# Identity products, idle rings and a lead for attention ahead of the first FFN tiles

## The chip, the cores and the metric

One NeuronCore of a Trainium2 chip runs the whole program. The metric is the device time of one execution in microseconds. TensorE is called PE in the profile (PEld for its weight loads), VectorE DVE, ScalarE ACT, GpSimd POOL and SyncE SP; SP here only issues DMAs.

## What is computed

Windowed attention with a few sink keys, then a mixing over the sequence and a two-layer FFN, for 4 batches of 768 positions with 8 heads of 64.

```python
scores = q @ k.T / 8                  # kept: the first 4 keys, and the last 128 up to the query
a = softmax(scores)                   # with 1e-9 added to the denominator
x = (a @ v) as [4, 768, 512]
h = x^T @ U @ V                       # U [768, 32], V [32, 768]
u = x + h^T
out = u + relu(u @ w_ch1) @ w_ch2     # w_ch1 [512, 2048], w_ch2 [2048, 512]
```

All arrays are fp32. Most products run in a faster fp32 format ("fp32r") on an operand split in two, a high part and the remainder, so that one fp32 product becomes three: weights as `w` (high and low), activations as `uh` and `ul`, hidden values as `hh` and `hl`. Some products of batch 0 and 1 run in plain fp32 on unsplit operands; the code calls those "whole" or "native".

## The kernel before

Rows are taken in blocks of 128 and in two chunks (halves) of 384 positions. The work of a batch:

- *Attention*, per head and half: scores (`scores`, L637 to L641) into a PSUM bank, mask and row minimum on DVE (L643), exponential with the row sum on ACT (L648), the division (`normalise`: `r` by L667 and L669, then the scaling L679 to L682), transposes of the probabilities (`transposes`, L701), and the values (`values`, L751), which end in `xT`, x with channels on the partitions.
- *Loads of v* (`prep_v`): for "whole" heads (all 16 of batch 0, all 8 of batch 1) v goes straight from memory into a buffer of the ring `vhl`, which has two.
- *Mixing*: when a half's heads are done, `mix_half` transposes each block of x (L865), copies it to `xf` (a helper's line, L462), multiplies it by U into the bank `tp` (L871) and stores it in `xd`, from where the FFN's last step fetches it. The ring `xf` has two buffers, shared with the first loads (hence the names first1q and first1k). `mix_end` then copies `tp` to `t` (L462, L912). For each chunk c and each of four channel groups d it forms the mixing in a bank, adds it to x and splits the sum into `uh` and `ul`. In batch 0 the contribution of the sink keys is a separate product (L922) into the same bank, ahead of the product with `t` (L925).
- *FFN* (`ffn`): per tile f of 128 hidden units, 12 products of `uh`, `ul` with `w` (L952 to L954), the ReLU split in `hh` and `hl` (L960, L963), and 9 products into three accumulating banks (L973). The accumulators start with the mixing itself (L990, in batch 0 with L987 ahead of it), so x alone is left to be added at the end (L999).
- *Weights*: each of the 16 tiles is split once, in batch 0. `narrow` takes a raw piece through a row of DVE and ACT steps (L94 to L102) and `weights` writes high and low part (L462, L469). Two tiles stay resident, the other 14 share four buffers and are written to memory and fetched back. In batch 0 the FFN goes through the tiles in groups of four, chunk 1 first (`FLIP = 1`), then chunk 0 with the same four backwards and the next four, and so on.

The order of the instructions on every engine is not written out. `Plan` schedules all steps on a model before anything is emitted: each step has a duration for each engine that may run it, a priority `prio`, and the tiles it reads and writes; of the ready steps the one with the lowest priority number goes first on a free engine. Where a step may run on several engines, `any` lets the plan choose, with the durations weighted by `PRICE`. The order is refined in up to ten rounds of a backward and a forward pass:

```python
for s in self.steps:
    s.prio = -s.back - s.lead
```

`lead` is what stands in `plan.lead` when a step is made: `LEAD0` for the attention and mixing of batch 0, 0 for the splitting of weights and the FFN, `LEAD` = 30 for the attention of later batches. Tile buffers come from rings: box i of a ring may be used once box i - n has been read for the last time, and its first step stands behind the first step of box i - 1. PSUM banks are a free pool of eight. All loads and stores go through SP's one queue in the plan's order.

Of the kernel before, what the change touches and what calls it, by code (L numbers as in the profile page):

```python
# [10 lines left out]
F32R = mybir.dt.float32r  # L11
# [10 lines left out]
P = 128  # L22
# [36 lines left out]
PERIOD = 4.32  # L59
ACC = (0xFFFF, 0xFFFF, 0xFFFF, 0xFFFF)  # L60
WHOLE = {0: (0xFFFF, 0xFFFF), 1: (0xFF, 0xFF)}
LEAD0 = 0.0
LEAD = 30.0
BESIDE = ((6, 2.5), (0, 2.5), (0, 2.5))
ORDER = (0, 1, 2, 3, 4, 5, 6, 7, 8, 9, 10, 11, 12, 13, 14, 15)
# [369 lines left out]
class Fast:  # L435
# [135 lines left out]
    def prep_v(self, b, h, blocks, t0, whole=False):  # L571

        nc, add = self.nc, self.plan.add
        k0, k1 = blocks
        n = k1 - k0
        src = lambda: self.v[b, h][:, k0:k1, :]
        if whole:
            t = self.vhl()
            flat = lambda: f32(t().rearrange("p n s d -> p (n s d)")[:, :(n + 1) * D])
            self.put(t, lambda: (flat().rearrange("p (n d) -> p n d", n=n + 1), self.v[b, h][:, k0:k1 + 1, :]), (n + 1) * 32768, t0 - 8)  # L580
            return t, flat, k0
        r, t = self.v_raw(), self.vhl()
        self.put(r, lambda: (r()[:, :n], src()), n * 32768, t0 - 8)
        self.copy(n * D, lambda: t()[:, :n, 0, :], lambda: r()[:, :n], r=(r,), w=(t,), prio=t0 + 3)
        self.tt(n * D, lambda: t()[:, :n, 1, :], lambda: r()[:, :n], lambda: f32(t()[:, :n, 0, :]), ALU.subtract,
                r=(r,), w=(t,), prio=t0 + 3)
        return t, None, k0
# [75 lines left out]
    def normalise(self, b, h, half, t0, acc, p, sm, psink):  # L663
        nc, add = self.nc, self.plan.add
        r = self.rr()
        if acc:
            add("DVE", 0.08, lambda: nc.vector.scalar_tensor_tensor(  # L667
                r(), sm(), 1e-9, sm(), ALU.add, ALU.max), r=(sm,), w=(r,), prio=t0)
        add("DVE", 0.09, lambda: nc.vector.reciprocal(r(), r() if acc else sm()), r=(sm,), w=(r,), prio=t0)  # L669
        kept = lambda: p()[:, :, SW:]  # L670
        by = lambda: r().unsqueeze(2).broadcast_to([P, NBLK, SW])
# [149 lines left out]
    def mix_half(self, b, half, t0):  # L821
# [38 lines left out]
        for blk in range(half * NBLK, (half + 1) * NBLK):  # L860
            xp = self.bank()

            def mms(xp=xp, blk=blk):
                for pr in range(NPAIR):
                    nc.tensor.transpose(  # L865
                        xp()[:, pr * P:(pr + 1) * P], xT[pr]()[:, blk * P:(blk + 1) * P], self.ident)
            add("PE", mm(P, NPAIR), mms, r=[(x, (half, i)) for x in xT for i in range(2)], w=(xp,), prio=t0)
            xf = self.xf()
            self.copy(DM, xf, xp, psum=True, r=(xp,), w=(xf,), prio=t0)
            if native:  # L870
                add("PE", mm(DM, 4), lambda blk=blk, xf=xf: nc.tensor.matmul(  # L871
                    tp(), self.usf()[:, blk, :], xf(),
                    start=blk == 0, stop=blk == NB - 1), r=(xf, self.T[b], self.usf), w=(tp,), prio=t0)
                xd = self.xd[b][blk]
                self.put(xd, lambda xd=xd, xf=xf: (xd(), xf()), 262144, t0, r=(xf,))
                continue
            xh, xl = self.xh(), self.xl()
            self.copy(DM, xh, xf, r=(xf,), w=(xh,), prio=t0)
            self.tt(DM, xl, xf, lambda xh=xh: f32(xh()), ALU.subtract, r=(xf, xh), w=(xl,), prio=t0)
            xd = self.xd[b][blk]  # L880
            self.put(xd, lambda xd=xd, xf=xf: (xd(), xf()), 262144, t0, r=(xf,))

            def st1(blk=blk, xh=xh, xl=xl):
                nc.tensor.matmul(tp(), self.ust()[:, blk, :], xh(), start=blk == 0, stop=False)
                nc.tensor.matmul(tp(), self.ust()[:, blk, :], xl(), start=False, stop=blk == NB - 1)
            add("PE", mm(DM, 2), st1, r=(xh, xl, self.T[b], self.ust), w=(tp,), prio=t0)
# [21 lines left out]
    def mix_end(self, b, t0):  # L908
# [5 lines left out]
        for c in range(NCHUNK):  # L914
            uh, ul = self.u[b, c] = self.uh(), self.ul()
            sl = slice(c * CH, (c + 1) * CH)
            for d in range(NC):
                pu, x = self.bank(), xT[d]
                parts = [(x, (c, j)) for j in range(2)]
                if b == 0:  # L920
                    pst, vs = self.late[3][c], self.late[4]
                    add("PE", mm(CH), lambda pu=pu, d=d, vs=vs, pst=pst: nc.tensor.matmul(  # L922
                        pu()[:, :CH], vs()[:, d, :], pst()[:, :CH], start=True, stop=False),
                        r=(vs, pst, x), w=(pu,), prio=t0)
                add("PE", mm(CH), lambda pu=pu, d=d, sl=sl: nc.tensor.matmul(  # L925
                    pu()[:, :CH], t()[:, d * P:(d + 1) * P], self.vst()[:, sl], start=b > 0, stop=True),
                    r=(t, self.vst), w=(pu,), prio=t0)
                add("DVE", dve(CH), lambda pu=pu, x=x, sl=sl: nc.vector.tensor_tensor(
                    x()[:, sl], x()[:, sl], pu()[:, :CH], ALU.add), r=(pu,), w=parts, prio=t0)
                top = lambda uh=uh, d=d: uh()[:, d, :]  # L930
# [5 lines left out]
    def ffn(self, b, c, fs, prio, first, begin=True, end=True):  # L936
# [40 lines left out]
        for i in range(n + 1):  # L977
            if i < n:
                l1(i)
            if i == 0:  # L980
                acc = [Box(lambda i: self.banks[i], self.accs[k:k + 1], ring=self.bank) for k in range(NBLK)]
                self.accs = acc
                for k in range(NBLK if begin else 0):
                    blk = c * NBLK + k
                    if b == 0:
                        pst, vs = self.late[3][c], self.late[4]
                        add("PE", mm(DM), lambda k=k, vs=vs, pst=pst: nc.tensor.matmul(  # L987
                            acc[k](), pst()[:, k * P:(k + 1) * P], vs().rearrange("p n d -> p (n d)"),
                            start=True, stop=False), r=(vs, pst), w=(acc[k],), prio=prio)
                    add("PE", mm(DM), lambda k=k, blk=blk: nc.tensor.matmul(  # L990
                        acc[k](), self.vst()[:, blk * P:(blk + 1) * P], self.T[b](), start=b > 0, stop=False),
                        r=(self.vst, self.T[b]), w=(acc[k],), prio=prio)
# [362 lines left out]
```

## Time and profile before

| | |
|---|---|
| time, median of 3 runs (lowest to highest) | 780.61 us (780.37 to 783.29) |
| the profiled execution | 780.66 us, span 778.9 us |
| busy share PE / DVE / ACT / POOL | 97% / 60% / 45% / 30% |
| granted TensorE clock, mean | 0.990 |
| DMA | 153.90 MB, mean 198 GB/s |

A busy PE is not PE at its peak, since matmuls are pipelined; rows of a timeline can overlap for that reason. The idle time before an instruction, in brackets, is put down to the semaphore event that came last; where the engine named had long been done, it was another, often a DMA. Helpers record many operations under one line (copies L462 and L463, elementwise L469 and L471), so such rows are told apart by their tiles.

### The profile page before, as it was taken

What the parts mean: (1) busy time and instruction counts of PE and PEld (TensorE: products, weight loads), DVE (VectorE), ACT (ScalarE), POOL (GpSimd) and SP (SyncE); (2) the same over time, 40 slices, a digit from 0 to 9 for tenths busy, and PEclk for the clock granted to TensorE, in tenths of its full rate; (3) what the DMA queues carried; (4) which work ended last, traced back from release to release, by engine and by line L of the source; (5) the groups of instructions that cost most, each with busy time, mean ns of one, the idle gap of its engine ahead of it and who ended that gap; (6) DMA issues with size and microseconds to landing.
All of it is one profiled execution on the core that took longest, in us unless ns stands there. A gap on an engine that the chain in (4) does not pass through costs nothing.

```text
span 778.9 us, 11763 instructions
## 1 busy us (share of the span) xinstructions
PE 754.1 (97%) x4004; PEld 668.9 (86%) x4004; DVE 468.8 (60%) x1205; ACT 352.7 (45%) x953; POOL 233.6 (30%) x332
## 2 busy tenths in 40 slices
PE   8897899999999999999999999999999999999996
PEld 6675788888888899999889998899999899898995
DVE  8999649889889767866864157676754131112111
ACT  6996327566567454645642144545642111111110
POOL 5662104222233444655811035356521000000000
PEclk9999799999999999999999999999999999999999
DMA  8797448785595729764477529853147536533652
GB/s 292 255 315 272 148 149 285 227 266 183 175 284 197 262 76 277 248 203 129 121 229 252 186 76 271 233 177 132 68 129 250 204 135 222 207 112 121 243 195 93
DMA packets 46981, 153.90 MB, mean 198 GB/s; under 512 B 5824, under 2 KB 13888, under 8 KB 37440
## 3 DMA queue, kind: packets, MB, share of 16 engines
q1 hardware_dynamic: 46752, 152.86, 59.8%
q8 instruction: 33, 0.54, 0.3%
q14 instruction: 36, 0.29, 0.1%
q10 hardware_dynamic: 160, 0.20, 0.1%
HBM read 123.42 MB, written 29.62 MB: 196 GB/s over the span
## 4 chain that ended last, share of the span: by engine, by line
PE 73%; DVE 15%; DMA 4%; ACT 4%; issue 2%; POOL 1%; SPq 0%; DVEq 0%; ACTq 0%; POOLq 0%
PE bank L973 29%; PE bank L952 10%; PE bank L954 10%; PE bank L953 10%; PE bank L751 4%; DMA qkraw<-in_q_dram 3%; DVE p L643 2%; PE bank L701 2%; DVE nr L99 2%; PE bank L637 1%; PE bank L640 1%; DVE bank L101 1%; DVE w L469 1%; PE bank L641 1%; DMA xd<-first1q 1%
## 5 line engine op out<-in xcount | busy, mean ns | idle before, releaser
L973 PE MATMUL bank<-w,hh 128*128 128x512 f32 x768 | 243.0, 398 | 0.0
L963 DVE SCALAR_TENSOR_TENSOR hl<-bank,hh 128x384 fp32r<-128x384 f32 x128 | 71.0, 554 | 197.9 <-ACT hh L960 197.3
L952 PE MATMUL bank<-ul,w 128*128 128x384 f32 x512 | 178.4, 348 | 0.3 <-DVE ul L469 0.2
L954 PE MATMUL bank<-uh,w 128*128 128x384 f32 x512 | 172.7, 337 | 0.0
L953 PE MATMUL bank<-uh,w 128*128 128x384 f32 x512 | 172.4, 337 | 0.0
L960 ACT ACTIVATE hh<-bank 128x384 fp32r<-128x384 f32 x114 | 55.9, 490 | 227.9 <-PE bank L954 227.0
L973 PEld LDWEIGHTS bank<-w,hh 128*128 128x128 f32 x768 | 139.9, 188 | 19.8
L973 PE MATMUL bank<-w,hl 128*128 128x512 f32 x384 | 152.0, 396 | 0.0
L648 ACT ACTIVATE p<-p,mn 128x260 f32<-128x260 f32 (+1 forms) x192 | 93.9, 491 | 48.8 <-DVE mn L643 48.0
L952 PEld LDWEIGHTS bank<-ul,w 128*128 128x128 f32 x512 | 96.4, 188 | 6.3 <-DVE ul L469 0.5
L953 PEld LDWEIGHTS bank<-uh,w 128*128 128x128 f32 x512 | 96.3, 188 | 5.6 <-DVE w L469 0.3
L471 POOL TENSOR_TENSOR p<-p 128x256 f32<-128x256 f32 (+1 forms) x48 | 42.4, 883 | 186.9 <-ACT p L648 186.3
L954 PEld LDWEIGHTS bank<-uh,w 128*128 128x128 f32 x512 | 96.1, 188 | 0.0
L973 PEld LDWEIGHTS bank<-w,hl 128*128 128x128 f32 x384 | 72.1, 188 | 17.0 <-DVE hl L963 0.3
L643 DVE CUSTOM_DVE_ANT_0 p<-bank,mask 128x260 f32<-128x260 f32 (+1 forms) x192 | 71.5, 400 | 24.2 <-PE bank L641 21.9
L751 PEld LDWEIGHTS bank<-oph,vhl 128*128 128x128 f32 x336 | 56.1, 193 | 16.0 <-POOL oph L726 3.8
L751 PE MATMUL bank<-oph,vhl 128*128 128x256 f32 (+1 forms) x336 | 62.8, 321 | 5.9 <-DVE nr L99 2.1
L726 POOL TENSOR_SCALAR_AFFINE_SELECT oph<-oph 128x384 f32<-128x384 f32 (+1 forms) x64 | 37.2, 582 | 22.9 <-ACT oph L462 19.7
L471 POOL TENSOR_TENSOR ul<-xT,uh 128x384 fp32r<-128x384 f32 x14 | 14.0, 1019 | 97.5 <-ACT uh L462 97.4
L701 PE MATMUL bank<-ident,p 128*128 128x128 f32 x192 | 34.3, 281 | 3.3 <-ACT p L679 2.5
L667 DVE SCALAR_TENSOR_TENSOR r<-sm 128x3 f32<-128x3 f32 x64 | 34.4, 538 | 4.8 <-ACT p L648 4.7
L701 PEld LDWEIGHTS bank<-ident,p 128*128 128x128 f32 x192 | 24.5, 142 | 13.9 <-ACT p L679 6.2
(171 smaller groups left out, 1077.8 us busy)
## 6 DMA issues: line engine op xcount, KB each, us to landing
w<-wd SPq DMA_DIRECT2D x60, 1024.0 KB, 4.9
big<-in_w_dram SPq DMA_DIRECT2D x32, 512.0 KB, 5.3
wd<-w SPq DMA_DIRECT2D x14, 1024.0 KB, 4.7
big<-xd SPq DMA_DIRECT2D x33, 256.0 KB, 3.7
qkraw<-in_q_dram SPq DMA_DIRECT2D x39, 192.0 KB, 5.0
qkraw<-in_k_dram SPq DMA_DIRECT2D x32, 198.0 KB, 4.9
out_dram<-big SPq DMA_DIRECT2D x24, 256.0 KB, 2.0
v_raw<-in_v_dram SPq DMA_DIRECT2D x16, 192.0 KB, 2.6
```

Of the source, the lines that this page charges most:

```text
L471: ways["POOL"] = (gps(n), lambda: nc.gpsimd.tensor_tensor(dst(), a(), b(), op), True)
L643: add("DVE", dve(wd), lambda st=st, u=u, lo=lo, wd=wd, qb=qb: nc.vector.tensor_tensor_reduce(p()[:, u, NS + lo:], st()[:, :wd], self.mask[ ...
L648: add("ACT", act(wd) + 0.22, lambda u=u, lo=lo: nc.scalar.activation(p()[:, u, NS + lo:], p()[:, u, NS + lo:], AF.Exp, bias=mn()[:, u:u + ...
L701: nc.tensor.transpose(tr()[:, u * P:(u + 1) * P], p()[:, u, SW + NS:], self.ident)
L726: add("POOL", 0.126 + CH * 0.914e-3, lambda t=t: nc.gpsimd.affine_select(as_(t()[:, :, 1, :]), f32(t()[:, :, 1, :]), [[0, NBLK], [1, P]], ...
L751: nc.tensor.matmul(out, st, f32(mv) if whole else mv, start=part == 0 and i == 0, stop=part == len(t) - 1 and i == len(mms) - 1, skip_grou ...
L952: nc.tensor.matmul(ph()[:, :CH], wh, ul()[:, d, :], start=d == 0, stop=False)
L953: nc.tensor.matmul(ph()[:, :CH], wl, uh()[:, d, :], start=False, stop=False)
L954: nc.tensor.matmul(ph()[:, :CH], wh, uh()[:, d, :], start=False, stop=d == NC - 1)
L960: self.plan.any({"ACT": (act(CH), lambda: nc.scalar.activation(hh(), ph()[:, :CH], AF.Relu)), "DVE": (dve(CH), lambda: nc.vector.tensor_sc ...
L963: add("DVE", dve(CH), lambda: nc.vector.scalar_tensor_tensor(hl(), ph()[:, :CH], 0.0, f32(hh()), ALU.max, ALU.subtract), r=(ph, hh), w=(hl ...
L973: nc.tensor.matmul(acc[k](), a()[:, sl], w()[:, m, :], start=not begin and i == 0 and j == 0, stop=i == n - 1 and j == 2)
```

## The change

There are seven edits, nearly all for batch 0.

1. `LEAD0` goes from 0 to 10.
2. The direct loads of v for odd heads go to the ring `opl` (two buffers), which holds the low part of transposed probabilities and stands idle while heads are "whole". This holds for batch 0 and for batch 1.
3. The step L667, `r` = row sum + 1e-9, may run on ACT, priced at 0.2 us, or on DVE, priced at 0.4 us instead of 0.08 and marked as one that shares a port with POOL.
4. In batch 0 the third block of each half (2 and 5) takes its `xf` from the ring `opl`.
5. In `mix_end` the sinks' product and the product with `t` become one step, so the first waits for `t` as well (batch 0, both chunks).
6. For batch 0's chunk 1 a product of x with the unit matrix (`ident`, plain fp32) opens the bank, with `tp` as an added dependency. `uh` is then copied from the bank and `ul` subtracted from it. x itself isn't updated.
7. In `ffn` the sinks' product into the accumulators (L987) waits for `T[b]`, the tile `t`.

```diff
-LEAD0 = 0.0
+LEAD0 = 10.0
@@ prep_v
-            t = self.vhl()
+            t = self.opl() if h % 2 else self.vhl()
@@ normalise
-            add("DVE", 0.08, lambda: nc.vector.scalar_tensor_tensor(
-                r(), sm(), 1e-9, sm(), ALU.add, ALU.max), r=(sm,), w=(r,), prio=t0)
+            self.plan.any({"ACT": (0.2, lambda: nc.scalar.activation(r(), sm(), AF.Copy, bias=1e-9)),
+                           "DVE": (0.4, lambda: nc.vector.scalar_tensor_tensor(
+                               r(), sm(), 1e-9, sm(), ALU.add, ALU.max), True)}, r=(sm,), w=(r,), prio=t0)
@@ mix_half
-            xf = self.xf()
+            if native and blk % NBLK == 2:
+                xf = self.opl(...)
+            else:
+                xf = self.xf()
@@ mix_end
-                if b == 0:
-                    pst, vs = self.late[3][c], self.late[4]
-                    add("PE", mm(CH), lambda pu=pu, d=d, vs=vs, pst=pst: nc.tensor.matmul(
-                        pu()[:, :CH], vs()[:, d, :], pst()[:, :CH], start=True, stop=False),
-                        r=(vs, pst, x), w=(pu,), prio=t0)
-                add("PE", mm(CH), lambda pu=pu, d=d, sl=sl: nc.tensor.matmul(
-                    pu()[:, :CH], t()[:, d * P:(d + 1) * P], self.vst()[:, sl], start=b > 0, stop=True),
-                    r=(t, self.vst), w=(pu,), prio=t0)
+                late = [self.late[4], self.late[3][c]] if b == 0 else []
+                early = b == 0 and c == FLIP
+                if early:
+                    add("PE", mm(CH, 4), lambda pu=pu, x=x, sl=sl: nc.tensor.matmul(
+                        pu()[:, :CH], self.ident, x()[:, sl], start=True, stop=False), r=parts + [tp], w=(pu,), prio=t0)
+
+                def run(pu=pu, d=d, sl=sl, late=late, early=early):
+                    if late:
+                        nc.tensor.matmul(pu()[:, :CH], late[0]()[:, d, :], late[1]()[:, :CH], start=not early, stop=False)
+                    nc.tensor.matmul(pu()[:, :CH], t()[:, d * P:(d + 1) * P], self.vst()[:, sl], start=not late, stop=True)
+                add("PE", mm(CH, 2 if late else 1), run, r=[t, self.vst] + late, w=(pu,), prio=t0)
+                if early:
+                    top, xs = lambda uh=uh, d=d: uh()[:, d, :], lambda pu=pu: pu()[:, :CH]
+                    self.copy(CH, top, xs, psum=True, r=(pu,), w=((uh, d),), prio=t0)
+                    self.tt(CH, lambda ul=ul, d=d: ul()[:, d, :], xs, lambda top=top: f32(top()), ALU.subtract,
+                            pool=False, r=(pu, (uh, d)), w=((ul, d),), prio=t0)
+                    continue
@@ ffn
-                            start=True, stop=False), r=(vs, pst), w=(acc[k],), prio=prio)
+                            start=True, stop=False), r=(vs, pst, self.T[b]), w=(acc[k],), prio=prio)
```

More of the change, by code (lines that the diff above doesn't have):

```diff
@@ L867, in mix_half @@
             add("PE", mm(P, NPAIR), mms, r=[(x, (half, i)) for x in xT for i in range(2)], w=(xp,), prio=t0)
-            xf = self.xf()
+            if native and blk % NBLK == 2:
+                xf = self.opl(lambda: f32(self.pool.tile([P, NBLK, 2, P], F32R, name="opl", bufs=NOP)).rearrange(
+                    "p n a b -> p (n a b)")[:, :DM])
+            else:
+                xf = self.xf()
             self.copy(DM, xf, xp, psum=True, r=(xp,), w=(xf,), prio=t0)
```

## The prediction

> **What bounds the kernel now.** I read the page's chain of waits first, then the engines' busy time by stage, and last the timeline of each engine around the start of the FFN. The chain that ended last looks settled: it is mostly TensorE's own.
>
> ```profile
> PE 73%; DVE 15%; DMA 4%; ACT 4%; issue 2%; POOL 1%; SPq 0%; DVEq 0%; ACTq 0%; POOLq 0%
> ```
>
> An average over stages hides the one that matters. The windows below cut the span at the points where the work changes: attention of batch 0 (10 to 71 us), its mixing (71 to 88), the first FFN tiles (88 to 110), FFN beside the rest of the weight splitting (110 to 262), and the rest. The columns are the length, then busy us and instructions for PE, PEld, DVE, ACT and POOL, the granted TensorE clock, and DMA.
>
> ```profile
> core 0 of [0], span 778.9 us
> core 0: us, PE busy (x) PEld busy (x) DVE busy (x) ACT busy (x) POOL busy (x), PEclk, DMA share, GB/s
> 10.00:71.00 61.00, 53.04 (x285) 43.53 (x285) 58.14 (x197) 53.81 (x170) 37.40 (x53) 0.97 0.86 295
> 71.00:88.00 17.00, 12.33 (x38) 8.16 (x37) 11.16 (x22) 7.37 (x15) 2.82 (x3) 0.70 0.74 268
> 88.00:110.00 22.00, 21.72 (x109) 19.39 (x109) 11.71 (x23) 5.39 (x11) 0.16 (x1) 1.00 0.12 43
> 110.00:262.00 152.00, 150.50 (x786) 131.62 (x785) 136.89 (x343) 99.02 (x252) 43.00 (x54) 1.00 0.73 235
> 262.00:779.00 517.00, 508.32 (x2764) 459.31 (x2762) 243.74 (x591) 182.45 (x495) 147.79 (x205) 1.00 0.55 179
> ```
>
> From 88 us on TensorE is the bound (508.3 of 517.0 us in the last window, the end of the span included). Work moved on other engines there is worth almost nothing. Before 88 us it is not: in 10 to 71 VectorE is 95% busy and ScalarE 88%, and in 71 to 88 nothing is full and the clock was only 0.70. So this change, nearly all of which lies in batch 0, is worth what it moves the first FFN product forward, less whatever TensorE work is only put off past that point.
>
> **The mixing, 71 to 88 us.** These are rows of TensorE's, ScalarE's, VectorE's and SyncE's timelines: start, us, engine, line, operation, and in brackets the idle time before.
>
> ```profile
> 73.88 0.60 PE L865 MATMUL bank<-ident,xT 128*128 128x128 f32 x4
> 79.00 0.69 PE L922 MATMUL bank<-xhl,vsh 128*128 128x384 f32 x1 [3.44 <-DVE w L469]
> 79.49 1.91 PE L871 MATMUL bank<-first1k,xT 128*128 128x512 f32 x2
> 88.22 0.44 PE L952 MATMUL bank<-ul,w 128*128 128x384 f32 x1
> ```
>
> ```profile
> 77.64 0.59 ACT L462 CAST w<-bank 128x512 fp32r<-128x512 f32 x1 [2.40 <-DVE bank L102]
> 78.12 0.59 ACT L462 COPY first1k<-bank 128x512 f32<-128x512 f32 x1
> 81.43 0.59 ACT L462 CAST t<-bank 128x512 fp32r<-128x512 f32 x1 [2.72 <-PE bank L871]
> ```
>
> ```profile
> 78.26 0.69 DVE L469 TENSOR_TENSOR w<-bank,w 128x512 fp32r<-128x512 f32 x1 [0.65 <-ACT w L462]
> 82.05 0.69 DVE L912 TENSOR_TENSOR t<-bank,t 32x512 fp32r<-32x512 f32 x1 [3.10 <-ACT t L462]
> ```
>
> ```profile
> 73.45 0.46 SPq L477 DMA_DIRECT2D xd<-first1k  x1
> xd<-first1k SPq DMA_DIRECT2D x3, 256.0 KB, 4.1
> ```
>
> The transposes of the last block end at 74.48. Its copy to SBUF starts only at 78.12: the two-deep `xf` ring still holds block 3 in first1k, whose store was issued at 73.45 and takes 4.1 us, to about 77.55. ScalarE does a weight copy in between. TensorE meanwhile sits 3.44 us before an L922 that waits for a PSUM bank, ahead of L871 in its order. The last L871 follows at about 79.7, `t` is complete at 82.74, and the first FFN product starts at 88.22. The profile's clock in fine windows over the end of this:
>
> ```profile
> 77.60:81.00 3.40, 2.00 (x4) 1.15 (x4) 0.70 (x2) 1.07 (x2) 0.00 (x0) 0.50 0.42 170
> 81.00:84.40 3.40, 2.43 (x7) 1.60 (x6) 1.57 (x3) 0.88 (x2) 0.00 (x0) 0.50 1.01 330
> ```
>
> What TensorE does here runs at half clock.
>
> What the edit does to it. Block 5 (and block 2) gets an idle `opl` buffer, so its copy no longer waits for the store. The L922 products are fused with the L925 ones and the accumulators' L987 wait for `t`, so neither holds a bank nor stands ahead of L871. Chunk 1, which the FFN takes first, gets four unit-matrix products (`ident` by x, fp32) after the last L871; then uh is copied from PSUM and ul subtracted from PSUM, without the L928 addition to x. Prices:
>
> ```profile
> 55.19 1.02 PE L871 MATMUL bank<-first1k,xT 128*128 128x512 f32 x2
> L462 ACT CAST oph<-bank 128x384 fp32r<-128x384 f32 x32 | 15.3, 478 | 6.0 <-PE bank L701 5.4
> L469 DVE TENSOR_TENSOR opl<-bank,oph 128x384 fp32r<-128x384 f32 x32 | 17.4, 552 | 2.9 <-ACT oph L462 2.0 <-POOL opl L726 0.5 <-ACT psink L690 0.2
> L928 DVE TENSOR_TENSOR xT<-xT,bank 128x384 f32<-128x384 f32 x32 | 15.5, 551 | 4.0 <-PE bank L925 3.7
> 90.17 0.17 PE bank L953
> 93.17 2.09 PE bank L973 x9
> ```
>
> An fp32 product with 512 columns took 1.02 us at full clock (two records), so one with 384 costs 0.7 (0.77 by proportion, less the overlap with its successor); four cost 2.8, which is new TensorE work. They run while `t` is copied and corrected (0.59 + 0.69 + about 0.2 of handoffs = 1.5 us, otherwise idle), so 1.3 of the 2.8 shows. An L922 and L925 pair is two 384-column products at the 0.17 us of the chain's row below the prices. After: copy 0.59, L871 1.0, identities 2.8, pair 0.4, uh 0.48, ul 0.55, four handoffs of about 0.1: 6.2 us from the transposes' end to the first FFN product, against 88.22 - 74.48 = 13.7. That is 7.5 us sooner. But all 16 L922 and L925 products of both chunks ran before 88.22 in the old order; the eight of chunk 0 are now put off into the stage that TensorE bounds, 8 x 0.17 = 1.4 us. L987 and L990 of chunk 1 (six 512-column products) fit in the wait for ul. Chunk 0's L928 and its uh and ul go into a VectorE that is 53% busy from 88 to 110; without that cover four additions would cost 2.2 us. The term is **-6.1 us**; its ends are -8 (chunk 0 fits in the waits too) and -2.3 (the clock stays at half, below).
>
> **The attention of batch 0, 10 to 71 us.** Three edits act here, and none has a row of its own, so I bound them together.
>
> ```profile
> 59.85 2.25 PE L751 MATMUL bank<-oph,vhl 128*128 128x128 f32 x8 [2.11 <-DVE nr L99]
> 52.84 0.64 SPq L477 DMA_DIRECT2D vhl<-in_v_dram  x1
> 28.00 1.32 PE L751 MATMUL bank<-oph,vhl 128*128 128x256 f32 x6 [0.93 <-DMA vhl<-in_v_dram]
> ...
> L667 DVE SCALAR_TENSOR_TENSOR r<-sm x64: 148/420/1804, 10.1 to 561.8; 128x3 f32<-128x3 f32 x64
> L667 DVE SCALAR_TENSOR_TENSOR r<-sm 128x3 f32<-128x3 f32 x16 | 6.2, 387 | 1.5 <-ACT p L648 1.5
> L690 ACT COPY psink<-p 128x12 f32<-128x12 f32 x9 | 1.7, 193 | 1.8 <-POOL p L681 1.8
> ```
>
> *v in the idle ring.* With two `vhl` buffers a load waits for the values two heads before. The 2.11 us before L751 at 59.85 is put down to a VectorE step, but the v load for that head was issued only at 52.84; I read it as that load landing. With the 0.93 at 28.00 this is 3.0 us of TensorE waiting that four buffers can end. The ring has a catch: `opl` is handed out in program order, so half 1's odd heads come behind block 2's copy, and head 3's buffer is the one block 2's store has to leave. SyncE's queue, in order, would hold the loads behind it: up to 4.1 us, though even heads can go first.
>
> *L667 to ScalarE.* On VectorE 16 of them took 6.2 us before 71 us; the nearest ScalarE row, a tiny copy, is 0.193, so 3.1 us there. The shortest L667 of the run took 0.148 us, so 16 x 0.148 = 2.4 is its own work and 3.8 is waiting inside it. Between 2.4 and 6.2 I take 2.4 as VectorE's gain, since a wait for something shared falls on the step behind, and 1 of ScalarE's 3.1 us as showing. In the Trainium skill, "SBUF — State Buffer", section "SBUF: two separate sides", a VectorE operation with two SBUF inputs and a GpSimd operation that reads SBUF lock each other out for a whole instruction; by that rule the 3.8 us passes to the next such step, and the gain is 2.4. The 148 to 1804 ns of one fixed shape agrees with it.
>
> *LEAD0 = 10* puts batch 0's attention ahead of weight splitting due up to 10 us earlier. VectorE is 95% busy with both; whatever weight work leaves this stage shortens it, until ScalarE or TensorE fills. TensorE is idle 8 us in the window, so 8 is the most that all three can give; nothing (ScalarE takes over as the bound) is the least. I take 3.0 + 2.4 - 1 = 4.4 from the first two and 0.6 more for the lead: **-5 us**, nearer the middle because the waits seen account for most of it.
>
> **What is late next: the weight tiles.** The FFN's first four tiles need their weights split, and the lead pushes that back.
>
> ```profile
> L96 DVE TENSOR_SCALAR nr<-nr 128x512 bf16<-128x512 bf16 x32 | 12.5, 390 | 2.5 <-ACT nr L95 2.4
> L99 DVE SCALAR_TENSOR_TENSOR nr<-big,nr 128x512 uint16<-128x512 uint16 x32 | 25.2, 788 | 3.1 <-ACT nr L98 2.4
> L101 DVE SCALAR_TENSOR_TENSOR bank<-big,nr 128x512 f32<-128x512 uint32 x32 | 23.3, 730 | 0.6
> L102 DVE TENSOR_TENSOR bank<-nr,bank 128x512 f32<-128x512 bf16 x32 | 22.0, 688 | 0.2
> L469 DVE TENSOR_TENSOR w<-bank,w 128x512 fp32r<-128x512 f32 x32 | 21.9, 686 | 2.9 <-ACT w L462 2.8
> ```
>
> A tile has two such pieces: at least 2 x 3.28 = 6.6 us of VectorE, while the FFN uses one per 4.2 us (12 products of 0.17 and the 9 of 2.09 in all). Before, the fourth was done at 78.95; five halves of 2.1 us go ahead of its first use, so it was wanted 11 us after the FFN's start and had 20 us in hand. A start 11 us sooner plus 10 us of lead uses that up, so I charge **+1 us** (ends 0 and the third rival). In 110 to 262 VectorE is 90% busy, but that stage moves forward whole and L667 leaves VectorE there too; I price the rest of the span at nothing, its cover being TensorE's own 98% and an idle VectorE (244 of 517 us).
>
> Sum: -6.1 - 5 + 1 = -10.1 us. The profiled execution took 780.66 us (span 778.9 and 1.8 around it), 0.05 above the median of the runs, so **770.5**.
>
> **Rivals.**
> 1. *Only the mixing gains.* ScalarE, 88% busy before 71 us and given 3.1 us more, keeps attention where it is, or the loads behind block 2's store do. 780.66 - 6.1 + 1 = 775.6. For it: ScalarE's row. Against: weight copies leave ScalarE as well, with the lead.
> 2. *The clock stays at half through the mixing.* In the row at 79.49 two records of L871 took 1.91 us instead of 1.02. The identities would cost 5.3 rather than 2.8, L871 0.9 more and the pairs 0.4 more: 3.8 us, 774.3. For it: both windows at 0.50. Against: they follow a gap of 3.44 us that the edit removes. In the Trainium skill, "TensorE: Matmul & The Clock Gate", part 1, an idle window of about 3.4 us halves the clock and a busy one restores it; by that rule, and the trace agrees, removing the gap removes this case.
> 3. *Slower: the weights come too late.* If the lead left none of the first four tiles split when the FFN starts, the fourth would be ready 4 x (6.6 + 0.55 for the FFN's own hl step of L928's size) = 28.6 us after it and wanted after 11: 17.6 us of waiting, 780.66 - 11.1 + 17.6 = 787. With one ready it is 10.5 us and no change; it decides at less than one tile ready. For it: 6.6 against 4.2 us. Against: the 17 us of mixing leave VectorE a third idle, and the 20 us in hand.
> 4. *Given back later.* The order of everything after 110 us is drawn up anew, with VectorE at 90%; a few waits of 2 us there would leave 777 to 781, no change.
>
> **Numbers.** My forecast has a chance of 0.56, with its own range 765 to 774; the first rival 0.16, the second 0.08, the fourth 0.12, the third 0.08. What this kernel's measurement can tell from no change is about 0.5%, 3.9 us. The first three cases are faster by more than that: 0.80; same 0.12; slower 0.08. The range runs from 764 (attention gives its 8, the mixing its 8 and the weights cost nothing: 764.7) to 778.5, past both faster rivals and into the fourth.
>
> **What would show it.** First FFN product (L952's line) at 75 to 80 us instead of 88.2; no gap over 2 us on TensorE between the last transposes and it; the clock at 1.00 there; no L922-type product ahead of `t`; the `r` step on ScalarE near 0.2 us; no wait for v loads on TensorE; weight tiles 1 to 3 done after the FFN begins but before their use. The forecast is wrong if TensorE shows waits for `w` in the first 20 us of the FFN, or if the last values of attention still end near 70 us.

## The result and the profile after

The changed kernel took 762.62 us in the median of four runs (760.85 to 762.81), beside 781.64 for the kernel before in the same comparison: a ratio of 0.975, 95% interval 0.9724 to 0.9777. A second series gave 762.24 us and 0.9796 (0.978 to 0.9813). The forecast was 770.5 with a range down to 764.0: the sign was right, the size was not. The profiled execution, the fastest of the four, took 760.85 us, 19.8 less than the one before. Two executions of the series below, one of the kernel before (825.39 us) and one of b_plan_r_act (1488.54 us), were slow and are left out of every median.

These are the windows of the changed kernel, cut where those of before were cut: attention of batch 0, its mixing, the first FFN tiles, the FFN beside the weight splitting, the rest.

```profile
core 0 of [0], span 759.1 us
core 0: us, PE busy (x) PEld busy (x) DVE busy (x) ACT busy (x) POOL busy (x), PEclk, DMA share, GB/s
10.00:62.00 52.00, 49.54 (x275) 41.10 (x276) 47.67 (x172) 47.40 (x171) 32.94 (x47) 1.00 0.92 309
62.00:76.00 14.00, 12.87 (x55) 8.44 (x55) 13.74 (x29) 10.07 (x21) 1.54 (x2) 1.00 0.83 283
76.00:98.00 22.00, 22.00 (x113) 20.03 (x112) 16.45 (x32) 7.63 (x15) 1.49 (x2) 1.00 0.55 197
98.00:247.00 149.00, 147.70 (x782) 131.13 (x781) 131.73 (x338) 99.59 (x266) 37.35 (x44) 1.00 0.71 236
247.00:759.00 512.00, 505.82 (x2766) 459.90 (x2764) 242.34 (x583) 184.02 (x540) 112.14 (x177) 1.00 0.55 180
```

Attention is shorter, and TensorE's idle time in it went from 8 us to 2.5. In the mixing the clock is 1.00 where it was 0.70. The mixing is VectorE's now: 13.74 of 14.0 us. What the forecast had not expected are the last two rows, 149 us for 152 and 512 for 517.

TensorE's rows in the changed kernel (some left out), from the last values of batch 0 to the first FFN product (L752, L866, L876 and L966 are the L751, L865, L871 and L952 of before; L928 is the unit product, L933 and L934 the fused pair):

```profile
60.96 1.47 PE L752 MATMUL bank<-oph,opl 128*128 128x128 f32 x8
63.55 1.73 PE L866 MATMUL bank<-ident,xT 128*128 128x128 f32 x12
65.59 1.12 PE L876 MATMUL bank<-first1q,xT 128*128 128x512 f32 x2 [0.31 <-ACT first1q L462]
66.56 1.02 PE L876 MATMUL bank<-first1k,xT 128*128 128x512 f32 x2
67.42 1.02 PE L876 MATMUL bank<-opl,xT 128*128 128x512 f32 x2
68.27 2.74 PE L928 MATMUL bank<-xT,ident 128*128 128x384 f32 x8
70.56 0.63 PE L933 MATMUL bank<-xhl,vsh 128*128 128x384 f32 x1
72.00 0.45 PE L933 MATMUL bank<-xhl,vsh 128*128 128x384 f32 x1 [0.61 <-DVE w L469]
73.86 0.45 PE L933 MATMUL bank<-xhl,vsh 128*128 128x384 f32 x1 [0.17 <-DVE xT L942]
76.17 0.40 PE L1004 MATMUL bank<-t,vst 128*128 128x512 f32 x1
76.40 0.34 PE L966 MATMUL bank<-ul,w 128*128 128x384 f32 x1
```

The last values of the kernel before, then TensorE's last product, before and in the changed kernel:

```profile
68.89 1.57 PE L751 MATMUL bank<-oph,vhl 128*128 128x128 f32 x8 [0.71 <-DVE w L469]
772.32 0.40 PE L973 MATMUL bank<-w,hl 128*128 128x512 f32 x1
753.06 0.40 PE L987 MATMUL bank<-w,hl 128*128 128x512 f32 x1
```

The last values end at 62.4 (before 70.5), the last product with U at 68.4 (81.4), and the FFN starts at 76.40 (88.2). Of the 11.8 us, attention gave 8.1 and the mixing behind it 3.7. From the FFN's first product to TensorE's last one it took 684.5 us before and 677.1 after: another 7.4 us gained. The rest, 0.6, is around the two ends.

The waits of TensorE's weight loads for attention's steps from 88 to 640 us (us in total, how often, the longest); first the kernel before, then the changed one:

```profile
PEld bank L701 <- ACT p L679: 3.7, 13, 1.0
PEld bank L751 <- POOL oph L726: 2.9, 7, 1.2
PEld bank L701 <- POOL p L681: 1.8, 5, 0.4
```

```profile
PEld bank L702 <- ACT p L680: 1.3, 3, 1.0
PEld bank L752 <- POOL oph L727: 0.9, 3, 0.6
PEld bank L702 <- POOL p L682: 0.6, 2, 0.3
```

These rows fall from 8.4 us to 2.8, and all waits of the weight loads in that stretch from 15.0 to 6.3. Weight loads overlap products that are still running, so the 5.6 us between are not 5.6 of the 7.4: from the FFN's start to 640 us the products themselves stood still for 4.1 us before and for 1.9 after. What TensorE waits for in these rows is the scaled probabilities of batches 1 to 3 and what is made of them, and the division is a chain that begins with the step `r`. "TensorE is 98% busy" had hidden them.

### The profile page after: what moved, and what is told of

Its sections match the earlier page's. It is cut to its first block, busy times and chain, and to the rows that moved or that the text cites. A ratio compares the mean times of both kernels' runs of the same rounds, so it can differ in the third digit from the quotient of the medians.

```text
span 759.1 us, 11690 instructions
## 1 busy us (share of the span) xinstructions
PE 745.9 (98%) x4012; PEld 667.4 (88%) x4012; DVE 459.1 (60%) x1184; ACT 353.4 (47%) x1024; POOL 187.9 (25%) x288
## 4 chain that ended last, share of the span: by engine, by line
PE 91%; DVE 5%; ACT 2%; issue 1%; POOL 0%; DMA 0%; POOLq 0%; DVEq 0%
PE bank L987 35%; PE bank L966 12%; PE bank L968 12%; PE bank L967 12%; PE bank L752 6%; PE bank L637 4%; PE bank L702 2%; PE bank L640 2%; PE bank L641 1%; PE bank L866 1%; DVE bank L101 1%; PE bank L1004 1%; ACT p L648 1%; DVE p L469 1%; PE bank L849 1%
## 5 line engine op out<-in xcount | busy, mean ns | idle before, releaser
L987 PE MATMUL bank<-w,hh 128*128 128x512 f32 x768 | 243.4, 398 | 0.0
L966 PE MATMUL bank<-ul,w 128*128 128x384 f32 x512 | 178.9, 349 | 0.0
L974 ACT ACTIVATE hh<-bank 128x384 fp32r<-128x384 f32 x119 | 58.4, 491 | 220.8 <-PE bank L968 219.9
L987 PEld LDWEIGHTS bank<-w,hh 128*128 128x128 f32 x768 | 139.3, 188 | 19.4
L987 PE MATMUL bank<-w,hl 128*128 128x512 f32 x384 | 152.3, 397 | 0.0
L966 PEld LDWEIGHTS bank<-ul,w 128*128 128x128 f32 x512 | 96.2, 188 | 5.7
L987 PEld LDWEIGHTS bank<-w,hl 128*128 128x128 f32 x384 | 72.1, 188 | 17.7 <-DVE hl L977 1.1
L682 POOL TENSOR_TENSOR p<-p,r 128x396 f32<-128x396 f32 x33 | 29.0, 878 | 113.1 <-DVE r L670 95.9
L471 POOL TENSOR_TENSOR p<-p 128x256 f32<-128x256 f32 (+1 forms) x22 | 19.2, 871 | 81.2 <-ACT p L648 77.7
L752 PEld LDWEIGHTS bank<-oph,vhl 128*128 128x128 f32 x224 | 35.8, 190 | 3.9 <-POOL oph L727 0.6
L752 PE MATMUL bank<-oph,vhl 128*128 128x256 f32 (+1 forms) x224 | 38.9, 303 | 0.0
L648 ACT ACTIVATION_READ_ACCUMULATOR p<-p,mn 128x1 f32 x192 | 36.1, 188 | 0.0
```

Source lines behind the costliest of these rows:

```text
L471: ways["POOL"] = (gps(n), lambda: nc.gpsimd.tensor_tensor(dst(), a(), b(), op), True)
L648: add("ACT", act(wd) + 0.22, lambda u=u, lo=lo: nc.scalar.activation(p()[:, u, NS + lo:], p()[:, u, NS + lo:], AF.Exp, bias=mn()[:, u:u + ...
L752: nc.tensor.matmul(out, st, f32(mv) if whole else mv, start=part == 0 and i == 0, stop=part == len(t) - 1 and i == len(mms) - 1, skip_grou ...
L966: nc.tensor.matmul(ph()[:, :CH], wh, ul()[:, d, :], start=d == 0, stop=False)
L974: self.plan.any({"ACT": (act(CH), lambda: nc.scalar.activation(hh(), ph()[:, :CH], AF.Relu)), "DVE": (dve(CH), lambda: nc.vector.tensor_sc ...
L987: nc.tensor.matmul(acc[k](), a()[:, sl], w()[:, m, :], start=not begin and i == 0 and j == 0, stop=i == n - 1 and j == 2)
```

## The experiments

Two theories stood against each other on the stretch behind the FFN's start. One: the step `r` itself, which left VectorE for ScalarE in all four batches. The other: the order, which the plan draws anew after any edit. A third question was whether a part put in alone is worth almost nothing or whether the parts add up. The texts below call these theories 1 to 4, in this order. Kernels "on before" are the kernel before with one edit; the others are the changed kernel with one edit undone or altered. "Start" is the start of the first FFN product, "behind" the time from there to TensorE's last product, both worked out from rows of the profiled execution. The kernel before took 779.1 to 780.7 us beside these runs.

| kernel | median us | ratio, 95% | start | behind |
|---|---|---|---|---|
| before | 780.6 | | 88.2 | 684.5 |
| changed | 762.62 | 0.975 (0.9724 to 0.9777) | 76.4 | 677.1 |
| changed, again | 762.24 | 0.9796 (0.978 to 0.9813) | 77.6 | 677.2 |
| b_plan_r_act | 773.64 | 0.9901 (0.9863 to 0.9938) | 88.3 | 681.6 |
| a_plan_r_dve | 769.33 | 0.9852 (0.9819 to 0.9885) | 80.9 | 681.6 |
| a_plan_r_dve_late | 766.85 | 0.9834 (0.9815 to 0.9852) | 77.9 | 680.9 |
| a_no_r | 770.35 | 0.9866 (0.9844 to 0.9889) | 83.8 | 679.3 |
| b_r_only | 770.94 | 0.99 (0.9861 to 0.9939) | 89.1 | 674.4 |
| a_old_mix_end | 770.13 | 0.9878 (0.9851 to 0.9906) | 83.3 | 678.9 |
| a_no_ident | 764.06 | 0.9798 (0.9776 to 0.9819) | 79.2 | 677.2 |
| a_chunk0_late | 765.78 | 0.9832 (0.9815 to 0.9848) | 84.9 | 674.4 |
| b_mix_end | 775.78 | 0.9958 (0.9929 to 0.9987) | 85.7 | 683.7 |
| a_old_xf | 766.85 | 0.983 (0.9806 to 0.9854) | 81.8 | 676.7 |
| b_xf | 776.07 | 0.9959 (0.994 to 0.9979) | 84.1 | 683.8 |
| a_old_v | 768.49 | 0.9846 (0.9823 to 0.9868) | 83.9 | 677.2 |
| b_v | 774.40 | 0.9938 (0.9914 to 0.9962) | 83.7 | 684.7 |
| a_lead0 | 764.78 | 0.9791 (0.9768 to 0.9814) | 82.0 | 676.4 |
| a_lead9 | 766.05 | 0.9825 (0.9806 to 0.9844) | 81.2 | 676.7 |
| a_lead14 | 765.15 | 0.9813 (0.9791 to 0.9834) | 80.9 | 676.6 |
| b_lead10 | 776.37 | 0.9963 (0.9946 to 0.998) | 88.9 | 679.7 |

No run beat the changed kernel. The series ran on different chips, so medians of two of them compare to a microsecond or two only: the changed kernel itself is 19.0 us below the kernel before in one series and 16.9 in the other.

### The step r, with the order held

The plan's prices were kept as they were, so that the order stays, and only the engine that carries out the step was exchanged. On before:

```diff
-            add("DVE", 0.08, lambda: nc.vector.scalar_tensor_tensor(
-                r(), sm(), 1e-9, sm(), ALU.add, ALU.max), r=(sm,), w=(r,), prio=t0)
+            add("DVE", 0.08, lambda: nc.scalar.activation(r(), sm(), AF.Copy, bias=1e-9), r=(sm,), w=(r,), prio=t0)
```

> The kernel before with its order untouched (the plan still prices the step r as 0.08 us on VectorE), but the instruction emitted at that place runs on ScalarE. Theory 1 (the step r itself: 34.4 us of VectorE, most of it waiting behind GpSimd, held up the chain of every attention step): 772 to 775 us, most of the gain after the first FFN product, whose start moves 1 to 3 us. Theory 2 (the gain after the first FFN product comes from the new order drawn up with the new prices, not from where r runs): 779 to 782 us, waits after 90 us as before.

And the reverse on the changed kernel; the "late" one does it for batches 1 to 3 alone (`if b > 0`):

```diff
-            self.plan.any({"ACT": (0.2, lambda: nc.scalar.activation(r(), sm(), AF.Copy, bias=1e-9)),
+            self.plan.any({"ACT": (0.2, lambda: nc.vector.scalar_tensor_tensor(
+                               r(), sm(), 1e-9, sm(), ALU.add, ALU.max)),
```

> The changed kernel with its order untouched (the plan still prices the step r as 0.2 us on ScalarE), but the instruction emitted runs on VectorE as in the kernel before. Theory 1: 768 to 771 us. Theory 2: 762 to 765 us. The L667 rows on VectorE again show means near 0.4 to 0.5 us in either case.

> The changed kernel in its own order, with the instruction of the step r on VectorE in batches 1 to 3 alone. If the step holds up TensorE behind the FFN's start too: first FFN product at 76 to 77 us and 765 to 767 us, 3 to 4 us over the changed kernel. If r counts in batch 0 alone and the rest of the later gain is the new order: 762 to 764 us.

In the old order the move took 6.6 us off (780.28 to 773.64), in the new one 6.9 (769.33 to about 762.4). The two agree, with no other edit in play; by the ratios, each against its own series, the 6.9 lies between 4.4 and 8.0. Batches 1 to 3 alone are worth 4.4 of it, and the last column gives 3.7 (680.9 against 677.2) for them. The profiled execution of b_plan_r_act took 777.72, 4.1 over its median, so its 681.6 is rather too long.

In the old order the FFN's start did not move (88.25 against 88.22), where 1 to 3 us were expected. A row of b_plan_r_act suggests why:

```profile
60.13 2.00 PE L750 MATMUL bank<-oph,vhl 128*128 128x128 f32 x8 [2.80 <-DMA vhl<-in_v_dram]
```

With VectorE relieved, the wait that stood at 59.85 under a VectorE step's name is still there, under the name of the load of v, which bears out the forecast's reading. In batch 0 the move of `r` paid in the new order, where the v ring had been relieved too: with that order held, the FFN starts at 80.9 with the step on VectorE in all batches and at 77.9 with it on ScalarE in batch 0.

The step by shape: before, in b_plan_r_act, and in a_plan_r_dve.

```profile
L667 DVE SCALAR_TENSOR_TENSOR r<-sm 128x3 f32<-128x3 f32 x64 | 34.4, 538 | 4.8 <-ACT p L648 4.7
```

```profile
L667 ACT ACTIVATE r<-sm 128x3 f32<-128x3 f32 x64 | 12.6, 196 | 0.2
```

```profile
L667 DVE SCALAR_TENSOR_TENSOR r<-sm 128x3 f32<-128x3 f32 x64 | 23.1, 361 | 0.5 <-ACT p L648 0.5
```

What VectorE was freed of is read from the windows. First before, then b_plan_r_act, in the same order; VectorE is the third busy time.

```profile
0.00:90.00 90.00, 75.28 (x357) 59.84 (x358) 78.50 (x255) 66.96 (x198) 42.81 (x73) 0.92 0.81 277
90.00:640.00 550.00, 546.11 (x2987) 489.67 (x2987) 368.62 (x914) 270.41 (x724) 190.78 (x259) 1.00 0.60 191
```

```profile
0.00:90.00 90.00, 75.14 (x357) 59.85 (x357) 73.32 (x239) 68.17 (x214) 41.63 (x73) 0.92 0.81 277
90.00:640.00 550.00, 546.40 (x3002) 494.61 (x3003) 349.03 (x867) 274.29 (x773) 192.50 (x259) 1.00 0.59 192
```

In the first 90 us VectorE lost 5.2 of the 6.2 us that the step had taken there, and behind them 19.6 of 28.2: 24.8 of 34.4 in all. At the step's shortest time, 0.148 us, its own work would be 9.5 of the 34.4 and the waiting 24.9, of which 15.3 went. So most of the waiting inside the step did not pass to the next one.

TensorE's waits from 88 to 640 us in a_plan_r_dve_late, the new order with the step on VectorE in the later batches:

```profile
PEld bank L703 <- ACT p L681: 2.8, 8, 1.2
PEld bank L753 <- POOL oph L728: 1.3, 4, 0.6
PEld bank L703 <- POOL p L683: 1.3, 4, 0.7
```

They are 5.4 us, against 2.8 in the changed kernel and 8.4 before: the step accounts for about half of the waits that went. In the old order the move alone took them from 8.4 to 4.9. Over all twenty profiles the waits of the weight loads for `p`, `oph` and `opl` behind the FFN's start are 5.6 to 8.4 us in the eight kernels with this step on VectorE there, and 0.7 to 4.9 in the twelve with it on ScalarE.

### The step r, with the plan drawn anew

Edit 3 undone in the changed kernel, and edit 3 alone on before:

```diff
-            self.plan.any({"ACT": (0.2, ...), "DVE": (0.4, ..., True)}, r=(sm,), w=(r,), prio=t0)
+            add("DVE", 0.08, lambda: nc.vector.scalar_tensor_tensor(...), r=(sm,), w=(r,), prio=t0)
```

> The changed kernel with the step r as before (VectorE, priced 0.08 us), planned anew. If the step r is what gained 7 us, in any order: 768 to 772 us, with TensorE's time from the first FFN product to the end back at 681 to 685 us (677 in the changed kernel). If the gain behind the FFN's start needs the old order: 762 to 766 us.

> The kernel before with the edit of the step r alone, planned anew. Theory 1: 771 to 775 us with less TensorE waiting after 90 us. Theory 2: within 4 us of before either way, since it is one more order among many; no less TensorE waiting after 90 us in particular.

Against a_no_r (770.35) the new price without the move (a_plan_r_dve, 769.33) is worth 1.0 us, and on before the new price with the move (770.94) is 2.7 faster than the move alone (773.64). Both pairs of intervals overlap, so a gain from the new price is not shown; that from the move is. The new price does change who does what: GpSimd's busy time from 90 to 640 us is 190.78 before and 196 in a_no_r, but 148 to 156 in the three kernels drawn with the price (a_plan_r_dve, changed, b_r_only). From before to changed, 18.2 us of that are splits of `kl` and `qs`, which take about 0.98 us on VectorE and 1.9 on GpSimd, and 18.9 us are elementwise steps on `p`.

The last column of the table shows the same split: the six kernels drawn with the old price and with `r` on VectorE (before, a_no_r, b_lead10, b_xf, b_v, b_mix_end) take 679.3 to 684.7 us behind the FFN's start, the kernels drawn and run with `r` on ScalarE 674.4 to 678.9. b_r_only shows both sides of an order: with a_chunk0_late the shortest stretch behind (674.4), and no gain ahead of it, although there too `r` is off VectorE.

But an order alone can do much of it. b_lead10 and a_no_r, both with `r` on VectorE, take 679.7 and 679.3 behind, 4.8 and 5.2 less than before; for a_no_r 681 to 685 had been expected. So the 7.4 us have no single owner: with the order held `r` is worth 3.7 there, and without the move a new order comes close to 5.

### The end of the mixing

Edits 5 to 7 undone; the unit products alone left out; chunk 0's mixing given a lower priority; edits 5 to 7 alone on before:

```diff
@@ a_old_mix_end: edits 5 to 7 as in the kernel before; b_mix_end: these three on before
@@ a_no_ident
-                early = b == 0 and c == FLIP
+                early = False
@@ a_chunk0_late, in mix_end
+            if b == 0:
+                self.plan.lead = LEAD0 if c == FLIP else -10.0
```

> The changed kernel with the end of the mixing as before (no unit-matrix products, the sinks' products separate and not tied to t, the accumulators' first product not tied to t), the other edits kept. If the fused and early products carry the mixing's gain: 768 to 771 us with the first FFN product at 81 to 84 us. If the idle buffer for block 5 carries it: 763 to 766 us with the first FFN product at 77 to 79 us.

> The changed kernel without the unit-matrix products of chunk 1 (x gets the mixing by VectorE and is split as before), the fused products and the accumulators tied to t kept. My prediction's working: the products themselves cost 1.3 us more than they hide, and spare 0.55 + 0.5 us per channel group in the chain; 763 to 765 us. If the whole 7.5 us of the mixing's end are theirs: 769 to 771 us. If the fusing is what counts: 761 to 763 us.

> The changed kernel with the mixing of chunk 0 (its products, sums and splits) given a lead of -10 instead of 10, so that the FFN of chunk 1 need not stand behind it. If only put off, as my prediction had it: first FFN product 1 to 3 us sooner after the last product with U than the 8.0 us of the changed kernel, and no time won by it, 761 to 767 us with the order's own spread. If the waiting before the first FFN product is what costs: 758 to 761 us.

> The kernel before with the unit-matrix products, the fused products and the accumulators tied to t alone. Theory 3: 776 to 781 us, first FFN product at 84 to 88 us (the last block's copy still waits for its store). Theory 4: 773 to 776 us, first FFN product at 81 to 82 us. From there to the end as for the lead.

Without the three edits the changed kernel takes 7.5 us more. TensorE's rows and the windows of a_old_mix_end around the FFN's start:

```profile
77.87 0.50 PE L992 MATMUL bank<-vsh,xhl 128*128 128x512 f32 x1 [1.71 <-DVE t L917]
83.35 0.44 PE L957 MATMUL bank<-ul,w 128*128 128x384 f32 x1 [2.02 <-POOL ul L471]
```

```profile
83.40:86.00 2.60, 2.60 (x10) 2.60 (x11) 2.60 (x7) 0.17 (x1) 0.00 (x0) 0.61 0.19 71
86.00:90.00 4.00, 4.00 (x20) 3.87 (x19) 2.24 (x5) 1.58 (x4) 0.00 (x0) 0.83 0.42 131
```

TensorE waits for `t` and then for `ul`, and the FFN begins at 0.61 of the clock. From the last product with U to the FFN took 7.4 us here and 8.0 in the changed kernel: the loss is not in that stretch. Behind the FFN's start it is 1.8 us (678.9 against 677.1), with the clock down. The rest lies ahead: attention's last values end at 68.9 instead of 62.4, where those of the kernels with another lead end too (67.2 to 68.2). How much of the 7.5 belongs to the three edits and how much to the draw of the order is therefore not shown. b_mix_end, drawn anew too, is 3.3 us below the kernel before; its 775.78 us fit theory 4, its start of 85.7 theory 3.

The unit products alone are not told from nothing in time: 764.06 against 762.62 and 762.24, with ratios of 0.9798 against 0.975 and 0.9796. In the profile the stretch from the last product with U to the FFN takes 9.1 us without them and 8.0 with them. Their place is seen in a_no_ident, in rows and windows over the wait for `t`:

```profile
73.81 0.69 PE L934 MATMUL bank<-vst,t 128*128 128x384 f32 x1 [3.56 <-DVE t L917]
```

```profile
70.00:73.50 3.50, 0.26 (x2) 0.00 (x0) 3.43 (x7) 2.37 (x5) 0.00 (x0) 0.97 0.81 230
73.50:76.50 3.00, 2.69 (x8) 2.69 (x9) 2.72 (x6) 1.24 (x4) 0.73 (x1) 0.50 1.00 382
```

Without them TensorE stands still for 3.56 us, and then the clock is 0.50. With them it is 1.00: work that fills the wait also keeps the clock. In the Trainium skill, "TensorE: Matmul & The Clock Gate", part 1, an idle window of about 3.4 us halves the clock; this trace agrees. In a_old_mix_end the clock fell to 0.61 although no wait just ahead of it was longer than 2.02 us, so one long wait is not needed for it.

In a_chunk0_late chunk 0's mixing was given a lower priority. It was 3.5 us slower than the changed kernel in the same comparison (765.78 against 762.24). But all eight pairs still stand ahead of its first FFN product, which comes 8.0 us after the last product with U as in the changed kernel, not 1 to 3 sooner; and attention's last values end at 71.9 instead of 62.4. So the products were not put off, and what the order that the forecast had assumed is worth stays untested.

### The two idle rings

Edit 4 and edit 2, each undone and each alone on before:

```diff
@@ a_old_xf (b_xf: the reverse, on before)
-            if native and blk % NBLK == 2:
-                xf = self.opl(...)
-            else:
-                xf = self.xf()
+            xf = self.xf()
@@ a_old_v (b_v: the reverse, on before)
-            t = self.opl() if h % 2 else self.vhl()
+            t = self.vhl()
```

> The changed kernel with the third block's xf back in its two-deep ring. My prediction's reading (the last block's copy waited 3.6 us for a store): first FFN product at 79 to 81 us instead of 76.4, 765 to 767 us. Rival (with the banks free, the copy is no longer late, and the store has landed): within 1 us of the changed kernel.

> The kernel before with the idle buffer for the third block's xf alone. Theory 3: 777 to 781 us, first FFN product at 85 to 88 us. Theory 4 (and my prediction's working, in which this removes 3.6 us and the half clock behind it): 774 to 777 us, first FFN product at 82 to 84 us. From there to the end as for the lead.

> The changed kernel with all loads of v in the two buffers of vhl. If the two-deep ring held up attention: TensorE waits for v loads again, 3 us in all, first FFN product at 79 to 80 us, 765 to 767 us. Rival (other work fills those waits, or the loads behind block 2's store cost as much): within 1.5 us of the changed kernel.

> The kernel before with the loads of v for odd heads in the idle ring alone. Theory 3: 777 to 781 us, first FFN product at 85 to 88 us. Theory 4: 773 to 776 us, first FFN product near 81. My prediction gave it 3 us. From there to the end as for the lead.

A wait came back at both places. First a_old_xf (TensorE, ScalarE and SyncE's queue), then a_old_v:

```profile
66.87 0.33 SPq L477 DMA_DIRECT2D xd<-first1k  x1
72.26 0.57 ACT L462 COPY first1k<-bank 128x512 f32<-128x512 f32 x1
72.88 1.13 PE L872 MATMUL bank<-first1k,xT 128*128 128x512 f32 x2 [4.00 <-ACT first1k L462]
```

```profile
67.84 1.55 PE L752 MATMUL bank<-oph,vhl 128*128 128x128 f32 x8 [2.42 <-DMA vhl<-in_v_dram]
```

In a_old_xf the third copy stands behind a store issued at 66.87, and TensorE loses 4.00 us; the kernel loses 4.2. In a_old_v a load of v holds TensorE for 2.42 us. That is less than the 5.9 us that the kernel loses, more than the expected 3: its last values end at 69.4, and the rest is not told from the draw. Alone on before the v ring ended the last values at 66.9 instead of 70.5, 3.6 sooner, and was worth 4.7 us, with the FFN's start at 83.7 where 81 was expected; the `xf` ring alone was worth 3.0.

### The lead, and how far the order is luck

LEAD0 at 0, 9 and 14 in the changed kernel, LEAD0 = 10 alone on before, and the changed kernel once more:

```diff
-LEAD0 = 10.0
+LEAD0 = 0.0     # a_lead0; 9.0 in a_lead9, 14.0 in a_lead14; b_lead10: 0 to 10 on before
```

> The changed kernel with LEAD0 = 0. My prediction gave the lead 0.6 us: within 2 us of the changed kernel. Rival (weight splitting on VectorE ahead of attention is what held the start): first FFN product at 80 to 84 us and weight tiles done earlier, 766 to 770 us.

> The changed kernel with LEAD0 = 9, which means nothing by itself but makes the plan draw up another order. If an order drawn at random is worth 2 to 3 us: 764 to 767 us. If the changed kernel's order is no better than its neighbours: 761.5 to 763.5 us.

> The changed kernel with LEAD0 = 14: a second order drawn anew, and the lead's effect if it still grows. If the start is held by VectorE's weight work yet: 759 to 761 us, first FFN product at 74 to 75 us. If the lead is spent, or the tiles now come late: 763 to 768 us.

> The kernel before with LEAD0 = 10 alone. Theory 3 (the start of the FFN stands at the end of several waits in a row or side by side, so a part taken out alone is worth 5 to 7 us but a part put in alone almost nothing): first FFN product at 86 to 89 us, 777 to 782 us. Theory 4 (the parts add up): 775 to 779 us with the first FFN product near 83. In either case the time from the first FFN product to the end, 684.5 us before, tells what a mere new order does there: 682 to 687 us if little, 675 to 680 us if the later gain is an accident of the order.

> The changed kernel once more, beside the next one on the same chip: 761 to 764 us, the first FFN product at 76 to 77 us. It gives the distance of the neighbours in LEAD0 and of the moved step r on a second chip.

The time does not follow the lead: 0, 9, 10 and 14 gave 764.78, 766.05, 762.6 and 765.15. A lead of 9 for 10 cannot matter by itself, and yet attention's last values end 4.8 us later (3.6 by the changed kernel's second profile). a_lead9's rows of values:

```profile
60.16 0.49 PE L752 MATMUL bank<-oph,opl 128*128 128x128 f32 x2 [1.42 <-DVE oph L711]
61.27 1.35 PE L752 MATMUL bank<-oph,opl 128*128 128x256 f32 x6 [0.62 <-POOL oph L727]
65.76 1.47 PE L752 MATMUL bank<-oph,opl 128*128 128x128 f32 x8
```

So 2 to 4 us of the changed kernel's gain seem to belong to a favourable draw of the order in batch 0. The ratios of these runs overlap with that of the changed kernel's second series; the starts, 80.9 to 82.0 against 76.4 and 77.6, do not. Behind the FFN's start the four leads differ by 0.7 (676.4 to 677.1). b_lead10 fits neither theory whole: 776.37 us as in theory 4, a start of 88.9 as in theory 3, and its 679.7 behind lies where a gain by the order's accident had been expected. That also bears on the sums. Undoing the edits one by one costs 7.7 (`r`), 7.5 (mixing), 5.9 (v), 4.2 (`xf`) and 2.2 (lead), 27.5 in all. In all of these but a_old_xf attention's last values end at 68.2 to 71.7, so the draw may be in each of them besides the edit. Adding them one by one to before, each against its own series, gives 9.3, 3.3, 4.7, 3.0 and 2.7, 23.0, somewhat more than the 16.9 to 19.0 of the whole. "One part alone is worth almost nothing" fell.

## Why the prediction was wrong, and where it was right

**The rest of the span priced at nothing: this step failed.** Its cover was named as "TensorE's own 98% and an idle VectorE". From the FFN's first product on, 7.4 us went. The cover was an average: TensorE's weight loads did wait there, 8.4 us in short waits for `p` and `oph`, and the row for L667 (x64, to 561.8 us) had shown the step in this stretch too, 48 times. The step itself in batches 1 to 3 is worth 4.4 us of the whole time with the order held, and 3.7 of this stretch. The other 3 to 3.7 go with the order; since b_lead10 and a_no_r gain 4.8 and 5.2 there without the move, the split holds for this order only, and what of it is luck stays open.

**Attention, -5: -8.1.** At the cap of 8 that the forecast gave. The v ring's 3.0 is near the 3.6 measured alone at the last values, though a new order by itself moves that point as far. The `r` step was sized too low on VectorE: its gain there was taken as 2.4 of 6.2 us, and 5.2 was measured. In time, batch 0's share is nothing in the old order, where the loads of v hold TensorE, and in the new one 6.9 - 4.4 = 2.5 us (3.0 by the FFN's starts), against the 2.4 - 1 = 1.4 forecast. The lead's 0.6 is not to be told from the draw, which moves this term by up to 5 us (67.2 against 62.4 with a lead of 9). So the size of this term is in part luck.

**Mixing, -6.1: -3.7 behind the last values.** The gap of 3.44 us and the half clock went, as forecast, and the four identity products, 2.3 us by the starts of L928 and L933, cover `t`. But the transposes' end (65.28) lies 11.1 us ahead of the first FFN product, not 6.2; from the 13.7 of before that is 2.6 less, and the other 1.1 lies between the values and the transposes. The forecast counted one product with U behind the transposes; all three blocks' stand there, 65.59 to 68.44. Chunk 0's work was not put off: all eight pairs stand ahead of the FFN. VectorE, nearly full, does chunk 0's four additions before chunk 1's `ul`, among weight steps:

```profile
70.21 0.69 DVE L917 TENSOR_TENSOR t<-bank,t 32x512 fp32r<-32x512 f32 x1
73.26 1.94 DVE L942 TENSOR_TENSOR xT<-xT,bank 128x384 f32<-128x384 f32 x4
75.12 0.55 DVE L469 TENSOR_TENSOR ul<-bank,uh 128x384 fp32r<-128x384 f32 x1
```

`t` is complete at 70.90, and the first `ul` starts only at 75.12. So 1.4 us of products were paid ahead of the FFN rather than behind it.

**Weights, +1: 0.** The fourth tile's last piece was done when the FFN was 9.4 us old, and its first use came at 86.9. From 76 to 98 us TensorE shows no wait at all.

```profile
85.09 0.69 DVE L469 TENSOR_TENSOR w<-bank,w 128x512 fp32r<-128x512 f32 x1 [0.65 <-ACT w L462]
```

**The signs named ahead.** The FFN's start at 75 to 80, no gap over 2 us, a clock of 1.00, `r` near 0.2 us on ScalarE, no v waits, the weights late but in time: all came. The one that did not quite is "no sinks' product ahead of `t`": the first L933 starts 0.34 us ahead, as the pair waits at its second product. The sum by stages thus was -8.1 - 3.7 + 0 - 7.4 - 0.6 = -19.8 against -6.1 - 5 + 1 = -10.1; errors of -3.1, +2.4 and -1 nearly cancelled ahead of the FFN, which is luck, and the 7.4 left out behind it made most of the miss. None of the rivals had it: all four looked for gains lost, none for a gain beyond batch 0.

## What to carry to other kernels

A step that leaves a busy engine in every batch is priced in every batch: look for the short waits of the bounding engine one by one and follow what makes them, before calling a stage covered by an average of 98%. Hold a planned order fixed and exchange the engine alone to price a step, and move a constant that cannot matter to see what a new order alone does; here that was 2 to 4 us of 762, as much as an edit. Idle rings paid where a row had shown the wait.

## What was not expected of the hardware

The step `r`, one fixed shape of 128x3, took 148 to 1804 ns on VectorE and 538 on average, and 187 to 213 on ScalarE. When it went, 24.8 of its 34.4 us on VectorE went too. In the Trainium skill, "SBUF — State Buffer", section "SBUF: two separate sides", a VectorE operation with two SBUF inputs and a GpSimd operation that reads SBUF lock each other out for a whole instruction. That the wait would then fall on the next step was the forecast's own inference, and the runs show that most of it did not. The lock itself no run here shows or excludes.
